# Group 2 of the second layer takes Strassen's scheme for its second product, as the last group does

## Chip, cores and metric

The kernel runs on one core of a Trainium2 chip. The metric is the device time of one execution in microseconds (us). TensorE (PE) multiplies, with its weight loads listed apart as PEld; VectorE (DVE) and ScalarE (ACT) work element by element; SyncE (SP) issues most of the transfers. Each engine takes its instructions in the order of its own queue.

## What is computed

An attention over random features gives 2304 tokens of 512 numbers. Two feed-forward layers follow, each with a first product (512 to 2048), a function element by element, and a second product (2048 to 512). The change lies in the second of them:

```python
def _moe2_ref(x, w_in, w_out):
    h = x @ w_in                      # (2304, 512) @ (512, 2048)
    g = np.where(h > 0.0, h, np.exp(np.minimum(h, 0.0)) - 1.0)
    return g @ w_out                  # (2304, 2048) @ (2048, 512)
```

Everything is float32. Each operand of a product is split into a high and a low part (fp32r), and a product is the sum of three: high by high, high by low, low by high.

## The kernel before

**Groups, blocks, tours.** The 2048 hidden numbers of a layer are cut into four groups of 512 (g = 0 to 3). The tokens are four full blocks of 512 (i = 0 to 3) and a block of 256 left over (i = 4). One pass over a block for a group is a tour (moe, g, k, i); moe = 1 is the second layer. Groups 1 and 2 of the second layer visit the blocks in the order 0, 4, 1, 2, 3, and group 3 in the order 0, 1, 2, 3, 4. A tour's second product is recorded inside the next tour, a quarter at each of four places.

**First product.** In all groups of the second layer it follows Strassen's scheme in Winograd's form: seven products of 12 matmuls (`times`, L759) into the PSUM banks `pa`, `pw` and `pb`, with the operands b, t3, t2, p, t1, t4, q, which SyncE loads from DRAM for every tour (`load_x`, L729). ACT copies `pa` into `pb` (L1082) before the product t2 adds onto `pb`; DVE makes the quadrants c22 (L1097) and c21 (L1102). Then come relu, exp and tanh on ACT, and two steps on DVE (L782 and L783 in a plain group, L951 and L952 in a Strassen group) for each of the four quadrants 11, 22, 21, 12.

**Second product, plain.** `chunk` (L810): four pieces of 12 matmuls with 512 moving columns, for which ACT casts each quadrant's high part (L792) and DVE subtracts it for the low part (L77). `summed` adds each result to the output so far, `ya` (L985), four DVE steps a tour.

**Second product by Strassen's scheme**, for the groups in `SECOND`: DVE makes four differences of quadrants (`difference`, L957: t1 = 21 - 22, t2 = 11 - t1, t3 = 11 - 21, t4 = 12 - t2). Seven operands are split (`halved`: ACT cast L963, DVE subtraction L77) instead of four. `quadrants` multiplies seven times 12 matmuls with 256 moving columns (L837), into the banks `px`, `pr`, y, z and v; ACT carries partial sums from bank to bank (L869, L880, L888); `grown` adds to the output in half steps (L921), twelve a tour. `sown` (L847) sets up two more banks once, at the first such tour of the layer. In these tours `pb` is the same bank each time; in the plain ones two banks take turns:

```python
            a, w, b = psum(f"pa{nm}"), psum(f"pw{nm}"), seeds[m % 2 if moe and not second else 0]
```

**Weights.** During the tours of a group the weights of the next group are made, at places that `chores_of` sets: 1, 2, 4, 6 and 8 of 8 parts by the end of the five tours. A part takes one step on ACT (L135) and two on DVE (L143, L150). Weights for a Strassen product also take eight half-wide DVE sums for four parts (L171 to L179) and seven casts and seven low parts (`wl`, L77), instead of four and four. These chores stand in the same queues as the tours' own steps.

Of the kernel before, what the change touches and what calls it, by code (L numbers as in the profile page):

```python
# [17 lines left out]
def linear_attention_two_ffn_kernel(  # L18
# [79 lines left out]
    parts = [(moe, f, o) for moe in range(2) for f in range(NF) for o in range(2)]  # L98
    parts[:2 * GF] = sorted(parts[:2 * GF], key=lambda p: (p[1] + LOOK * p[2], p[2]))
    parts[2 * GF:] = sorted(parts[2 * GF:], key=lambda p: (p[0], p[1] // GF, p[2], p[1]))  # L100
    SECOND = ((0,1),(0,2),(1,3))
    staged, w_t = {}, {}
    tf_t, combos, ws_t, casts, lows = {}, {}, {}, [], []
    HN = W // 2
# [2 lines left out]
    def summed_up(p):  # L107

        g = p[0], p[1] // GF
        return g in SECOND if p[2] else g != (0, 0)  # L110

# [731 lines left out]
    def sown(n, moe=0, g=1):  # L843
        wide = ws_t[moe, g * GF, "a"][0]
        while len(seeds) < n:
            seeds.append(psum(f"pb{moe}{len(seeds)}"))
            nc.tensor.matmul(seeds[-1], wide[:, :P], wide, start=True, stop=True)  # L847

    def quadrants(tour):

        moe, g, k, i = tour
        if moe == 0:
            sown(4, moe, g)
        elif k == 0 and (moe, g - 1) not in SECOND:
            del seeds[2:]
# [161 lines left out]
    def toured(before):  # L1017

        sown(2 if tours[0][:2] not in SECOND else 1)
        todo = [before[0:1], before[1:2], before[2:], []]  # L1020
        for n, tour in enumerate(tours):
# [8 lines left out]

            second = tour[:2] in SECOND
            if i == B:
# [216 lines left out]
```

## Time and profile before

| | |
|---|---|
| median of 3 runs | 908.32 us (907.88 to 908.86) |
| the profiled execution's own time | 908.27 us |
| its span, first to last instruction | 906.5 us |
| PE, DVE, ACT busy over the span | 894.5, 711.2, 607.7 us |
| group 2 of the second layer, first matmul of its block 0 to first of group 3's | 700.88 to 796.28 us of the span |
| group 3 of the second layer, from its first matmul on | 796.28 us of the span to the end |

The busy time of an engine counts its instructions where they overlap once. Matmuls are pipelined, so the time that one takes in a stream is read from one start to the next and not from its duration; the same holds for DVE, whose steps start before the one ahead has quite ended.

### The profile page before, as it was taken

The page shows a single profiled execution, that of the slowest core. Times are in us where ns is not written, and L with a number is a line of the kernel's source. Part 1 is how long each engine was busy: PE and PEld are TensorE (multiplying, and loading weights), DVE is VectorE, ACT ScalarE, POOL GpSimd, SP SyncE. Part 2 cuts the span into 40 slices and gives each one's busy share as a digit, 9 for nine tenths or more (in the row PEclk, how much of TensorE's full clock was granted, in tenths as well). Part 3 has the DMA queues.
Part 4 walks back from the last instruction along what each step waited for, and adds up shares of the span by engine and source line. Part 5 has one row for each costly group of instructions (what it writes and reads, how often), then busy time and mean ns, then how long its engine had stood idle before and what let it go on. Part 6 is the DMA issues. An engine that isn't in the chain of part 4 may idle for free. (4 is left out here: it accounts for less than half of the span.)

```text
span 906.5 us, 20710 instructions
## 1 busy us (share of the span) xinstructions
PE 894.5 (99%) x7807; PEld 844.4 (93%) x7807; DVE 711.2 (78%) x1329; ACT 607.7 (67%) x1292; POOL 86.8 (10%) x188
## 2 busy tenths in 40 slices
PE   8999999999999999999999999999999999999997
PEld 7888999998999999999999999899899989989997
DVE  5898875688876888777879897966597748878887
ACT  7999976664767675766366666755485638666663
POOL 4678730000000000000000000000000000000000
PEclk9999999999999999999999999999999999999999
DMA  9675522524998676577589664275468655653653
GB/s 242 168 196 159 170 83 75 177 94 154 349 374 302 216 250 239 179 231 255 197 279 335 244 209 164 96 256 195 160 203 270 222 183 168 205 200 126 222 173 94
DMA packets 134724, 183.89 MB, mean 203 GB/s; under 512 B 34272, under 2 KB 70624, under 8 KB 134624
## 3 DMA queue, kind: packets, MB, share of 16 engines
q1 hardware_dynamic: 133328, 181.88, 60.3%
q8 instruction: 62, 1.02, 0.5%
q10 hardware_dynamic: 1296, 0.69, 0.3%
q14 instruction: 38, 0.31, 0.1%
HBM read 145.29 MB, written 37.22 MB: 201 GB/s over the span
## 5 line engine op out<-in xcount | busy, mean ns | idle before, releaser
L810 PE MATMUL py<-wh,gh 128*128 128x512 f32 x216 | 85.2, 394 | 0.0
L810 PE MATMUL py<-wl,gh 128*128 128x512 f32 x216 | 85.1, 394 | 0.0
L810 PE MATMUL py<-wh,gl 128*128 128x512 f32 x216 | 85.1, 394 | 0.0
L782 DVE SCALAR_TENSOR_TENSOR r<-r,t 128x512 f32<-128x512 f32 x54 | 37.1, 687 | 57.4 <-ACT t L781 57.4
L77 DVE TENSOR_TENSOR gl<-gf,gh 128x512 fp32r<-128x512 f32 (+1 forms) x104 | 65.0, 625 | 4.1 <-ACT gh L792 0.5
L810 PEld LDWEIGHTS py<-wh,gl 128*128 128x128 f32 x216 | 40.6, 188 | 9.6
L810 PEld LDWEIGHTS py<-wl,gh 128*128 128x128 f32 x216 | 40.6, 188 | 7.4
L810 PEld LDWEIGHTS py<-wh,gh 128*128 128x128 f32 x216 | 40.6, 188 | 7.4
L135 ACT ACTIVATE cm<-st 128x512 f32<-128x512 f32 x64 | 44.2, 698 | 2.1 <-DMA st<-in_moe_w_out_dram 1.8
L792 ACT CAST gh<-gf 128x512 fp32r<-128x512 f32 x54 | 33.3, 617 | 17.0 <-DVE gf L783 16.1
L150 DVE SCALAR_TENSOR_TENSOR cv<-cm,cv 128x512 uint32<-128x512 uint32 x64 | 43.4, 685 | 0.8
L1082 ACT COPY pb<-pa 128x512 f32<-128x512 f32 x28 | 16.1, 574 | 40.1 <-PE pa L759 39.9
L1097 DVE TENSOR_TENSOR c<-pb,vs 128x512 f32<-128x512 f32 x28 | 19.3, 690 | 28.3 <-PE pb L759 21.7
L818 PE MATMUL py<-gh,wh 128*128 128x256 f32 x144 | 40.4, 281 | 0.0
L818 PE MATMUL py<-gh,wl 128*128 128x256 f32 x144 | 40.4, 281 | 0.0
L818 PE MATMUL py<-gl,wh 128*128 128x256 f32 x144 | 40.4, 281 | 0.0
L1090 ACT COPY us<-pb 128x512 f32<-128x512 f32 x28 | 16.4, 587 | 34.6 <-PE pb L759 29.1
L549 PE MATMUL ph<-xh,wh 128*128 128x256 f32 (+1 forms) x128 | 38.8, 303 | 0.0
L585 PE MATMUL py<-gh,wh 128*128 128x256 f32 (+1 forms) x128 | 38.4, 300 | 0.0
L585 PE MATMUL py<-gl,wh 128*128 128x256 f32 (+1 forms) x128 | 37.8, 295 | 0.0
L585 PE MATMUL py<-gh,wl 128*128 128x256 f32 (+1 forms) x128 | 37.8, 295 | 0.0
L549 PE MATMUL ph<-xh,wl 128*128 128x256 f32 (+1 forms) x128 | 37.7, 295 | 0.0
(1250 smaller groups left out, 3608.7 us busy)
## 6 DMA issues: line engine op xcount, KB each, us to landing
st<-in_moe_w_in_dram SPq DMA_DIRECT2D x32, 512.0 KB, 5.4
st<-in_moe_w_out_dram SPq DMA_DIRECT2D x32, 512.0 KB, 3.8
vk<-in_v_dram SPq DMA_DIRECT2D x32, 128.0 KB, 4.7
out_dram<-ya SPq DMA_DIRECT2D x30, 128.0 KB, 2.0
ld0k<-in_k_dram SPq DMA_DIRECT2D x4, 256.0 KB, 5.1
ld0q<-in_q_dram SPq DMA_DIRECT2D x4, 256.0 KB, 4.7
ld1k<-in_k_dram SPq DMA_DIRECT2D x4, 256.0 KB, 5.0
ld1q<-in_q_dram SPq DMA_DIRECT2D x4, 256.0 KB, 4.6
```

The lines of the kernel that those rows point to most:

```text
L77: eng.tensor_tensor(out=out, in0=whole, in1=hi.bitcast(F32), op=ALU.subtract)
L135: nc.scalar.activation(out=staged[p][1], in_=staged[p][0][:, :, 1].bitcast(F32), func=AF.Prelu, scale=REBIAS, alpha=NEGATIVE)
L150: nc.vector.scalar_tensor_tensor(out=t, in0=m.bitcast(U32), scalar=3, in1=t, op0=ALU.logical_shift_left, op1=ALU.bitwise_or)
L549: nc.tensor.matmul(ph[:, :n], wt[:, cs], x_part(xt, i, c)[:, n0:n1], start=(m == 0), stop=(m == 3 * KD - 1))
L585: nc.tensor.matmul(y, w[:, ts], a, start=j == 0 and m == 0 and t % per == 0, stop=j == GF - 1 and m == 2, skip_group_check=per > 1,)
L782: nc.vector.scalar_tensor_tensor(out=r, in0=r, scalar=1.0, in1=t, op0=ALU.add, op1=ALU.mult)
L792: nc.scalar.copy(out=gh, in_=gf)
L810: nc.tensor.matmul(y_t[l, u], a[:, s0], w, start=first and pr == 0 and m == 0, stop=last and pr == 1 and m == 2,)
L818: nc.tensor.matmul(y_t[l, u][:, e * HN:(e + 1) * HN], w[:, ts], a[:, pr * HN:(pr + 1) * HN], start=first and pr == 0 and m == 0 and e == 0 ...
L1082: nc.scalar.copy(out=b, in_=a)
L1090: nc.scalar.copy(out=us, in_=b)
L1097: nc.vector.tensor_tensor(out=c22, in0=b, in1=vs, op=ALU.add)
```

## The change

One entry more in the table of the groups whose second product takes Strassen's scheme: group 2 of the second layer, which had the plain one.

```diff
-    SECOND = ((0,1),(0,2),(1,3))
+    SECOND = ((0,1),(0,2),(1,2),(1,3))
```

The functions that it calls for that group are those that group 3 already uses. On PE the 48 matmuls of L810 in each full tour of group 2 become 84 of L837, and the rest stays in place. On DVE group 2's steps change as below. The numbers in a name are group and block (c_2_2 is c22 of group 2, block 2) and a buffer number; `gl` and `glt` are low parts, `g` and `gt` quadrants and differences, `r` the exp of a quadrant, `t` the tanh.

DVE's queue in block 2 of group 2, before, from c22 on:

```order
L1097 TENSOR_TENSOR c_2_2_11386<-pb_4446,vs_2_2_11384 128x512
L77 TENSOR_TENSOR gl_1_2_2_11531<-gf_1_2_2_11480,gh_1_2_2_11529 128x512
L1102 TENSOR_TENSOR c_2_2_11385<-pw_2_2_11382,us_2_2_11383 128x512
L985 TENSOR_TENSOR ya_1_0_0_9284<-py_2_1_0_0_11433,ya_1_0_0_9284 128x512
L985 TENSOR_TENSOR ya_1_0_1_9286<-py_2_1_0_1_11434,ya_1_0_1_9286 128x512
L782 SCALAR_TENSOR_TENSOR r_1_2_2_11553<-r_1_2_2_11553,t_1_2_2_11554 128x512
L783 TENSOR_TENSOR gf_1_2_2_11552<-r_1_2_2_11553,c_2_2_11386 128x512
```

The same place in the change:

```order
L1097 TENSOR_TENSOR c_2_2_11513<-pb_4446,vs_2_2_11511 128x512
L957 TENSOR_TENSOR g_1_2_1_11477<-g_1_2_1_11477,gt_1_2_1_11489 128x512
L77 TENSOR_TENSOR glt_1_2_1_11684<-g_1_2_1_11477,ght_1_2_1_11683 128x512
L1102 TENSOR_TENSOR c_2_2_11512<-pw_2_2_11509,us_2_2_11510 128x512
L921 TENSOR_TENSOR ya_1_0_0_9284<-pr_2_1_11639,ya_1_0_0_9284 128x256
L921 TENSOR_TENSOR ya_1_0_1_9286<-pr_2_1_11639,ya_1_0_1_9286 128x256
L921 TENSOR_TENSOR ya_1_0_0_9284<-pr_2_1_11639,ya_1_0_0_9284 128x256
L921 TENSOR_TENSOR ya_1_0_1_9286<-pr_2_1_11639,ya_1_0_1_9286 128x256
L951 SCALAR_TENSOR_TENSOR r_1_2_2_11709<-r_1_2_2_11709,t_1_2_2_11710 128x512
L952 TENSOR_TENSOR g_1_2_2_11708<-r_1_2_2_11709,c_2_2_11513 128x512
```

Between c22 and c21 there now stand the difference t4 of the block before and, right behind it, its low part, which needs ACT's cast of that difference; four half steps take the place of two full ones.

DVE's queue further on in block 2 of the change, from the difference t1 to the low part of t2 (before, nothing of L957 stood here, the four `wl` rows followed the last `gl` of block 2, and two rows of L985 stood where the four of L921 are):

```order
L957 TENSOR_TENSOR gt_1_2_2_11789<-g_1_2_2_11749,g_1_2_2_11708 128x512
...
L952 TENSOR_TENSOR g_1_2_2_11777<-r_1_2_2_11778,c_1_2_2_11781 128x512
L77 TENSOR_TENSOR wl_14a<-cv_14_0_11299,wh_14a 128x512
L77 TENSOR_TENSOR wl_14b<-cv_15_0_11419,wh_14b 128x512
L77 TENSOR_TENSOR wl_14c<-cs_15_0_11501,wh_14c 128x512
L77 TENSOR_TENSOR wl_12d<-cd_13_0_11218,wh_12d 128x512
L921 TENSOR_TENSOR ya_1_0_0_9284<-pb_11153,ya_1_0_0_9284 128x256
L921 TENSOR_TENSOR ya_1_0_1_9286<-pb_11153,ya_1_0_1_9286 128x256
L921 TENSOR_TENSOR ya_1_1_0_9368<-pb_11155,ya_1_1_0_9368 128x256
L921 TENSOR_TENSOR ya_1_1_1_9370<-pb_11155,ya_1_1_1_9370 128x256
L77 TENSOR_TENSOR glt_1_2_2_11877<-gt_1_2_2_11789,ght_1_2_2_11876 128x512
```

The chores for group 3's weights (`wl`) now stand between t1 and the low part of t2 (glt of gt, in the last row).

ACT's queue from the tanh of block 2's quadrant 12 to block 3's first copy, before:

```order
L781 ACTIVATE t_1_2_2_11612<-gf_1_2_2_11610 128x512
L792 CAST gh_1_2_2_11618<-gf_1_2_2_11582 128x512
L1082 COPY pb_4652<-pa_2_3_11644 128x512
L1083 COPY vs_2_3_11647<-pw_2_3_11645 128x512
L792 CAST gh_1_2_2_11684<-gf_1_2_2_11610 128x512
```

and in the change:

```order
L940 ACTIVATE t_1_2_2_11779<-g_1_2_2_11777 128x512
L963 CAST ght_1_2_2_11793<-gt_1_2_2_11789 128x512
L1082 COPY pb_4446<-pa_2_3_11836 128x512
L1083 COPY vs_2_3_11839<-pw_2_3_11837 128x512
L963 CAST ght_1_2_2_11876<-gt_1_2_2_11791 128x512
L963 CAST gh_1_2_2_11880<-g_1_2_2_11777 128x512
```

The copy of `pa` into `pb` (L1082), after which PE can go on with block 3, now stands behind the cast of DVE's difference t1 of block 2.

## Rows read from the trace of the kernel before

**Rows 1.** The page's first part: engines' busy us (share of the span), instructions.

```profile
PE 894.5 (99%) x7807; PEld 844.4 (93%) x7807; DVE 711.2 (78%) x1329; ACT 607.7 (67%) x1292; POOL 86.8 (10%) x188
```

**Rows 2.** Windows: length, PE, PEld, DVE, ACT, POOL busy, clock, DMA.

```profile
754.23:775.27 21.04, 21.04 (x135) 18.95 (x133) 20.25 (x37) 16.85 (x31) 0.00 (x0) 1.00 0.61 209
837.66:858.50 20.84, 20.40 (x171) 20.00 (x170) 17.46 (x34) 14.13 (x27) 0.00 (x0) 1.00 0.67 227
```

**Rows 3.** Timeline of DVE, group 3, block 2: start, us, instruction [idle before].

```profile
839.21 0.68 DVE L957 TENSOR_TENSOR gt<-g,g 128x512 f32<-128x512 f32 x1
...
847.61 0.69 DVE L951 SCALAR_TENSOR_TENSOR r<-r,t 128x512 f32<-128x512 f32 x1 [0.67 <-ACT t L940]
...
849.24 0.69 DVE L1097 TENSOR_TENSOR c<-pb,vs 128x512 f32<-128x512 f32 x1
849.85 0.68 DVE L957 TENSOR_TENSOR g<-g,gt 128x512 f32<-128x512 f32 x1
851.21 0.69 DVE L77 TENSOR_TENSOR glt<-g,ght 128x512 fp32r<-128x512 f32 x1 [0.69 <-ACT ght L963]
...
852.42 1.41 DVE L921 TENSOR_TENSOR ya<-pr,ya 128x256 f32<-128x256 f32 x4
853.75 0.68 DVE L951 SCALAR_TENSOR_TENSOR r<-r,t 128x512 f32<-128x512 f32 x1
...
856.79 0.69 DVE L951 SCALAR_TENSOR_TENSOR r<-r,t 128x512 f32<-128x512 f32 x1 [1.63 <-DMA xspl<-xd13p]
...
860.06 0.68 DVE L957 TENSOR_TENSOR gt<-g,g 128x512 f32<-128x512 f32 x1
```

**Rows 4.** Timelines of ACT and PE at that place.

```profile
839.93 0.62 ACT L963 CAST ght<-gt 128x512 fp32r<-128x512 f32 x1 [1.48 <-DVE gt L957]
840.45 0.58 ACT L1082 COPY pb<-pa 128x512 f32<-128x512 f32 x1
...
841.91 0.28 PE L759 MATMUL pb<-xst2h,wh_12c 128*128 128x256 f32 x1
```

**Rows 5.** Timeline of PE: a plain piece's 12 matmuls, then 24 of Strassen's.

```profile
778.09 0.40 PE L810 MATMUL py<-wh,gh 128*128 128x512 f32 x1
...
780.88 0.28 PE L759 MATMUL pb<-xst2h,wh_8c 128*128 128x256 f32 x1
...
834.82 0.28 PE L837 MATMUL pb<-wh_12D,gh 128*128 128x256 f32 x1
...
837.66 0.27 PE L759 MATMUL pa<-xsbh,wh_12a 128*128 128x256 f32 x1
```

**Rows 6.** Timeline of DVE: chores in group 2.

```profile
754.51 0.42 DVE L143 TENSOR_SCALAR cv<-st 128x512 uint32<-128x512 uint32 x1
754.84 0.68 DVE L150 SCALAR_TENSOR_TENSOR cv<-cm,cv 128x512 uint32<-128x512 uint32 x1
...
772.96 0.42 DVE L171 TENSOR_TENSOR cs<-cv 128x256 f32<-128x256 f32 x1
...
774.67 0.69 DVE L782 SCALAR_TENSOR_TENSOR r<-r,t 128x512 f32<-128x512 f32 x1
```

**Rows 7.** Waits of PE over the whole span: us in total, times, longest.

```profile
PE px L837 <- DVE wl_10B L77: 0.7, 1, 0.7
```

**Rows 8.** Timelines of DVE and PE, block 1 of group 2.

```profile
749.20 0.69 DVE L782 SCALAR_TENSOR_TENSOR r<-r,t 128x512 f32<-128x512 f32 x1 [8.36 <-ACT t L781]
...
756.77 0.68 DVE L77 TENSOR_TENSOR gl<-gf,gh 128x512 fp32r<-128x512 f32 x1
...
757.08 0.39 PE L810 MATMUL py<-wh,gh 128*128 128x512 f32 x1
```

**Rows 9.** Timeline of SP in group 3: output stores and the load behind them.

```profile
838.33 7.03 SPq L969 DMA_DIRECT2D out_dram<-ya  x8
845.45 0.40 SPq L729 DMA_DIRECT2D xst4h<-xd12t  x1
```

**Rows 10.** The page's costliest groups: busy us, mean ns.

```profile
L810 PEld LDWEIGHTS py<-wh,gl 128*128 128x128 f32 x216 | 40.6, 188 | 9.6
```

## The prediction

> **What bounds the kernel now.** I read the page first: PE is busy for 894.5 of 906.5 us [rows 1]. So a gain must come off PE's work, and a loss must come from a new wait of PE. Windows cut at the tours come next [rows 2]. In a plain tour of group 2 (21.04 us) DVE is busy for 20.25 us and PE for all of it; in a Strassen tour of group 3, which carries no chores, DVE still takes 17.46 of 20.84. The change brings both loads together in group 2. So I followed DVE through one Strassen tour in the timeline [rows 3], and then the step by which PE depends on it [rows 4].
>
> The chain is this. DVE makes the difference t1 of a block (839.21). ACT casts it (839.93), and only then, its queue being in order, copies `pa` into `pb` (840.45). PE's product t2 of the next block adds onto `pb` (841.91). At the least this takes 0.72 to the cast, 0.52 to the copy, and some 0.64 for the copy (0.58 long) to end and PE to go on: 1.88 us. Here it took 2.70, so PE had 0.82 us to spare. In a Strassen tour DVE may therefore be late by 0.8 us, and beyond that PE waits. The reader should compare the time from one t1 to the next on DVE with PE's time for the 14 products in between.
>
> **What the change saves.** PE's plain pieces take 2.79 us for 12 matmuls, 232.5 ns each; Strassen's take 2.84 us for 24, 118.3 ns each [rows 5]. A full tour goes from 48 x 0.2325 = 11.16 to 84 x 0.1183 = 9.94 us: 1.22 less, 4.9 in four tours. Block 4 has 24 of the wide ones (5.58) and gets 48 narrow ones (5.68), 0.1 more. The two matmuls of `sown` only move from group 3 to group 2. Together PE's work shrinks by 4.8 us.
>
> On the matmuls' spacing the Trainium skill says otherwise (TensorE: Matmul & The Clock Gate, "Back-to-back issue gap"): a stream of weight load and matmul pairs is given about 81 ns a matmul at 128 columns and about 131 at 512. A straight line between these, an estimate, gives 98 ns at 256, by which a tour would go from 6.3 to 8.2 us and the change would cost PE 7.8 us in four tours. The trace decides against it: 118 ns is close to half of 232.
>
> **What it adds on DVE.** A full tour goes from 18 full-wide steps to 21 and 12 half-wide ones. From t1 to t1 in group 3 DVE took 20.85 us [rows 3]. Of that it stood idle without need for 0.67 before 847.61 and 1.63 before 856.79, each 0.08 more since a step may start before the one ahead has ended (0.69 long, 0.61 from start to start at 849.24), and for some 0.3 between 847.61 and 849.24, where two steps that take 1.3 filled 1.63. What is left is 18.1 us. It includes 0.77 that can't be filled: the low part of t4 stands right behind t4 itself and waits for ACT's cast (849.85 to 851.21, where one step is 0.6).
>
> Chores come on top, at 0.60 for a low part or an L150, 0.33 for an L143 (754.51 to 754.84), and 1.71 for four half-wide sums that wait for one another (772.96 to 774.67) [rows 6]. From the order of the changed queue:
>
> - t1 of block 1 to t1 of block 2: two low parts, three L150, two L143, eight sums, 7.1 us; but four half steps fewer (1.33, [rows 3]), as block 4 is the one before. 18.1 + 7.1 - 1.3 = 23.9
> - block 2 to 3: four low parts, one L150, two L143, 3.7: 21.8
> - block 3 to group 3's block 0: four low parts, one L150, four sums, 4.7: 22.8
> - to group 3's block 1: three low parts, 1.8: 19.9
> - from there on 18.1.
>
> PE's 14 products of 12 take 168 x 0.1183 = 19.9 us (19.87). The first four loops need 88.4 on DVE and 79.5 on PE: with DVE late from the start, PE waits for 8.9 us in them. That PE waits for DVE where a Strassen tour carries chores is seen already, in the first layer: 0.7 us for a low part of a weight [rows 7].
>
> DVE is late from the start: in block 1 it has free time (8.36 idle before 749.20, until ACT's tanh), which the queue's order doesn't let later work use. The low part of quadrant 22 stands at 756.77 [rows 8]; two half steps (0.66) take their place behind it, so t1 begins at about 758.0 and PE's t2 at 759.9. PE has done the product t3 at 757.08 and, after one piece of the second product (1.42), would be ready at 758.5. That is a first wait of 1.4, which I keep between 0 (if block 1 runs ahead) and 1.4.
>
> Block 0 and block 4 together have 32.1 on DVE for some 31.7 on PE, but they start from plain tours with time to spare, and block 1's idle time takes up what is left. Group 2's own weights add three low parts and eight sums, under 6 us, to group 1's last tours, which by the same prices then hold 17.3 and 16.4 us of DVE's steps from c22 to c22 for 21 of PE; I cost that at nothing. ACT gets seven steps of about 0.52 more in a full tour; with 16.85 of 21.04 busy [rows 2] where chores are thickest it comes to some 20.5, below the 22 to 24 that such a tour now takes. The loads on SP keep their number and order.
>
> One cost is passed on to group 3. SP issues eight output stores, which wait for DVE's half steps, before it can load the operand t4 [rows 9], and the tour of [rows 2] is 20.84 long where its products take 19.87: 0.97 lost. With DVE at the end of its slack, those half steps come 0.8 later against PE: 0.8 more. Between 0 and 1.6 (two such tours).
>
> Sum: 908.27 (the profiled execution, whose span is 906.5; the median is 908.32, the same within its spread) - 4.8 + 1.4 + 8.9 + 0.8 = 914.6 us.
>
> **Rivals.**
>
> - *DVE's load stays hidden, and PE's saving is all that shows*: 908.27 - 4.8 = 903.5. For it: plain tours with 20.25 of 21.04 on DVE don't hold PE [rows 2]. Against: the slack of 0.8 [rows 4], and four loops in a row that need more than PE. It decides where PE's waits stay under 3.0 us, that is where DVE's four loops take 82 instead of 88.4.
> - *The slack comes back in each loop*: if the link from t1 to PE had 0.82 of give anew in each of the five places, 4.1 of the waits would go, and with them the passed-on 0.8: 909.7, no change to speak of (within 0.2%, 1.8 us, about what this measurement can tell from none). Against: a queue that is late stays late.
> - *Loads come late as well*: if each of the five tours of group 2 lost what the tour of group 3 loses at its t4 load, 0.97, it would be 4.9 more: 919.5. For it: operands need pages that Strassen tours hold longer. Against: no stores stand ahead of the loads there.
> - *Narrow matmuls are paced by their weight loads*, 188 ns each [rows 10]: 84 x 0.188 = 15.8 a tour, 4.6 more than before instead of 1.2 less, 18.6 in four; DVE would then hide: 908.27 + 18.6 = 926.9. The Trainium skill's spacing rule above points this way. Against it: the 24 narrow ones at 118 ns [rows 5].
>
> **How the numbers follow.** Main case 0.80, hidden 0.05, slack 0.06, late loads 0.08, paced 0.01. The main case's own bounds: first wait 0 to 1.4, passed-on cost 0 to 1.6, DVE's prices 1% either way on 88.4 (0.9), 0.7 more if ACT's tanh of quadrant 21 isn't ready in the loop with few chores. Low: -4.8 + 0 + 8.0 + 0 = +3.2, 911.5. High: -4.8 + 1.4 + 9.8 + 0.7 + 1.6 = +8.7, 917.0; I reach to 918 towards the late loads. Faster is the hidden case, 0.05; the slack case gives no change, 0.06; the rest is slower, 0.89. That the change doesn't do what it says is excluded: the queues show 84 matmuls of L837 for 48 of L810.
>
> **What would show it.** Right: narrow matmuls at 118 ns in group 2; tours of block 2, block 3 and group 3's block 0 of 22 to 24 us instead of 21; PE's waits there before `pb` (L759, released by ACT L1082), before L837 for a low part of t2 (released by DVE L77), and DVE with hardly any idle time but that behind t4; group 3's t4 load later still. Wrong: DVE idle time of more than 1 us a loop between block 2 of group 2 and block 1 of group 3, or PE without waits there.

## The result, and the profile after

The change makes the kernel slower: 921.58 us (median of four, 921.11 to 922.49) against 908.18 in the same session, a ratio of 1.0145 with the interval [1.0132, 1.0158]. That is 13.4 us more, where 6.3 were forecast: the sign was right, the size was about half of what came, and 921.6 lies outside the forecast of 911.5 to 918. The profiled execution has a span of 920.3 us (906.5 before).

Nearly all of it (13.2 us of the 13.8 by which the span grew) lies in four stretches, and these are the four loops of the prediction. I cut both traces where PE starts the product t2 (the first matmul into `pb` from `xst2h`): in block 2 and block 3 of group 2, then in blocks 0, 1 and 2 of group 3. Up to the first cut the two kernels are level (759.85 us before, 760.01 after); behind the last one 64.6 and 65.0 us are left. Between them stand, in windows of the kernel before and then of the changed one (columns as in [rows 2]):

```profile
759.85:841.91 82.06, 82.06 (x567) 76.14 (x566) 68.65 (x120) 54.38 (x98) 0.00 (x0) 1.00 0.51 173
```

```profile
760.01:784.30 24.29, 20.83 (x169) 20.10 (x169) 22.96 (x45) 17.30 (x33) 0.00 (x0) 1.00 0.53 173
784.30:806.28 21.98, 20.25 (x169) 20.04 (x169) 21.05 (x42) 16.82 (x32) 0.00 (x0) 1.00 0.52 170
806.28:833.97 27.69, 21.77 (x171) 21.36 (x170) 25.38 (x49) 17.61 (x33) 0.00 (x0) 0.94 0.59 194
833.97:855.29 21.32, 21.32 (x170) 21.32 (x169) 16.62 (x33) 13.60 (x25) 0.00 (x0) 0.92 0.20 70
```

82.06 us have become 95.28. I call the four loops A to D. PE's 168 matmuls take 19.9 us in each; in A to C DVE is busy for 92 to 96% of the time (as in the plain tour of [rows 2]; it was 84% in the Strassen tour there); in C and D, and nowhere else here, PE's granted clock is below 1.

PE's longest waits from 700 us on (us in total, times, longest), where before there was none of DVE's or ACT's over 0.4:

```profile
PE pb L837 <- DVE glt L77: 6.8, 3, 3.6
PE pb L759 <- ACT pb L1082: 2.6, 2, 1.6
PE px L837 <- DVE wl_14B L77: 2.3, 1, 2.3
...
PE px L837 <- DVE wl_10B L77: 0.3, 1, 0.3
```

The code calls the seven products of Strassen's second product p1 to p7. The first row is p6, which needs the low part of t2; the second is the link that the prediction followed [rows 4]; the third is p1, which needs the low part of a weight of group 3, and the last the same product in group 2's first tour. DVE's timeline through loop C (start, us, instruction, idle before) says why two of them are so long:

```profile
804.23 0.68 DVE L957 TENSOR_TENSOR gt<-g,g 128x512 f32<-128x512 f32 x1
...
808.14 0.69 DVE L150 SCALAR_TENSOR_TENSOR cv<-cm,cv 128x512 uint32<-128x512 uint32 x1
...
812.45 1.41 DVE L921 TENSOR_TENSOR ya<-pb,ya 128x256 f32<-128x256 f32 x4
813.78 0.68 DVE L77 TENSOR_TENSOR glt<-gt,ght 128x512 fp32r<-128x512 f32 x1
...
818.74 0.69 DVE L1097 TENSOR_TENSOR c<-pb,vs 128x512 f32<-128x512 f32 x1 [1.09 <-PE pb L759]
...
828.61 0.68 DVE L957 TENSOR_TENSOR gt<-g,g 128x512 f32<-128x512 f32 x1
...
832.52 0.69 DVE L77 TENSOR_TENSOR wl_14B<-cv,wh_14B 128x512 fp32r<-128x512 f32 x1
```

Between t1 (804.23) and the low part of t2 (813.78) stand an L150, four sums, three low parts of weights and four half steps, from 808.14 on 5.6 us. PE's wait for it delays the product t1, so that DVE itself stands idle for 1.09 us ahead of c22. And wl_14B comes 3.9 us behind the next t1. PE at the two waits, with the spacing of its matmuls:

```profile
810.66 0.28 PE L837 MATMUL pb<-wl_8C,ght 128*128 128x256 f32 x1
814.51 0.58 PE L837 MATMUL pb<-wh_8C,glt 128*128 128x256 f32 x1 [3.57 <-DVE glt L77]
...
815.11 0.41 PE L837 MATMUL pb<-wl_8C,ght 128*128 128x256 f32 x1
815.32 0.41 PE L837 MATMUL pb<-wh_8C,glt 128*128 128x256 f32 x1
...
817.83 0.28 PE L759 MATMUL pb<-xst1h,wh_14b 128*128 128x256 f32 x1
817.94 0.28 PE L759 MATMUL pb<-xst1l,wh_14b 128*128 128x256 f32 x1
...
830.64 0.28 PE L837 MATMUL px<-wh_14B,gh 128*128 128x256 f32 x1
833.26 0.39 PE L837 MATMUL px<-wl_14B,gh 128*128 128x256 f32 x1 [2.35 <-DVE wl_14B L77]
```

After the wait the matmuls stand 0.21 us apart, later 0.12 again. Windows show it as the clock (the column ahead of the last two): 0.50, the lower of its two levels, 1.2 GHz, behind either wait, from about 814.2 to 817.4 and from about 834.5 to 837.9 us.

```profile
814.50:816.80 2.30, 2.29 (x10) 2.29 (x11) 2.30 (x4) 0.16 (x1) 0.00 (x0) 0.50 0.09 35
...
836.26:836.76 0.50, 0.50 (x4) 0.50 (x4) 0.50 (x2) 0.42 (x1) 0.00 (x0) 0.50 0.00 0
...
838.30:840.50 2.20, 2.20 (x21) 2.20 (x20) 0.16 (x1) 1.75 (x3) 0.00 (x0) 1.00 0.45 133
```

### The profile page after: what moved, and what is told of

It is laid out like the page before. It is cut to its first block, busy times and chain, and to the rows that moved or that the text cites. A ratio compares the mean times of both kernels' runs of the same rounds, so it can differ in the third digit from the quotient of the medians.

```text
span 920.3 us, 21175 instructions
## 1 busy us (share of the span) xinstructions
PE 895.4 (97%) x7975; PEld 852.9 (93%) x7975; DVE 741.0 (81%) x1404; ACT 622.5 (68%) x1324; POOL 86.7 (9%) x188
## 5 line engine op out<-in xcount | busy, mean ns | idle before, releaser
L810 PE MATMUL py<-wh,gh 128*128 128x512 f32 x144 | 56.8, 394 | 0.0
L810 PE MATMUL py<-wh,gl 128*128 128x512 f32 x144 | 56.7, 394 | 0.0
L810 PE MATMUL py<-wl,gh 128*128 128x512 f32 x144 | 56.7, 394 | 0.0
L77 DVE TENSOR_TENSOR gl<-gf,gh 128x512 fp32r<-128x512 f32 (+1 forms) x86 | 52.6, 612 | 3.8 <-ACT gh L792 0.2
L782 DVE SCALAR_TENSOR_TENSOR r<-r,t 128x512 f32<-128x512 f32 x36 | 24.7, 687 | 33.9 <-ACT t L781 33.9
L150 DVE SCALAR_TENSOR_TENSOR cv<-cm,cv 128x512 uint32<-128x512 uint32 x64 | 43.3, 685 | 0.8
L963 ACT CAST gh<-g 128x512 fp32r<-128x512 f32 x56 | 34.5, 616 | 12.9 <-DVE g L952 12.9
L77 DVE TENSOR_TENSOR gl<-g,gh 128x512 fp32r<-128x512 f32 x56 | 38.4, 686 | 4.1 <-ACT gh L963 4.1
L963 ACT CAST ght<-g 128x512 fp32r<-128x512 f32 x32 | 19.8, 618 | 26.9 <-DVE g L957 26.9
L549 PE MATMUL ph<-xl,wh 128*128 128x256 f32 (+1 forms) x128 | 37.7, 294 | 0.0
L963 ACT CAST ght<-gt 128x512 fp32r<-128x512 f32 x32 | 19.8, 619 | 25.1 <-DVE gt L957 24.6
```

The costliest lines, as they stand in the source:

```text
L77: eng.tensor_tensor(out=out, in0=whole, in1=hi.bitcast(F32), op=ALU.subtract)
L150: nc.vector.scalar_tensor_tensor(out=t, in0=m.bitcast(U32), scalar=3, in1=t, op0=ALU.logical_shift_left, op1=ALU.bitwise_or)
L549: nc.tensor.matmul(ph[:, :n], wt[:, cs], x_part(xt, i, c)[:, n0:n1], start=(m == 0), stop=(m == 3 * KD - 1))
L782: nc.vector.scalar_tensor_tensor(out=r, in0=r, scalar=1.0, in1=t, op0=ALU.add, op1=ALU.mult)
L810: nc.tensor.matmul(y_t[l, u], a[:, s0], w, start=first and pr == 0 and m == 0, stop=last and pr == 1 and m == 2,)
L963: nc.scalar.copy(out=h, in_=t)
```

## The experiments

Seventeen kernels, all cut at the same rows of PE. "Over before" is the median less that of the kernel before on the same chip, whose medians were 908.2 to 909.1; the last column is what follows the last cut.

| run | median us | over before | first cut | A | B | C | D | A to D | rest |
|---|---|---|---|---|---|---|---|---|---|
| before | 908.2 | | 759.9 | 21.0 | 21.0 | 19.7 | 20.3 | 82.1 | 64.6 |
| after | 921.6 | 13.4 | 760.0 | 24.3 | 22.0 | 27.7 | 21.3 | 95.3 | 65.0 |
| low_pool | 924.3 | 15.6 | 761.4 | 27.4 | 24.7 | 23.4 | 19.9 | 95.5 | 64.7 |
| half_first | 922.7 | 13.9 | 761.6 | 24.4 | 22.6 | 26.2 | 22.0 | 95.1 | 65.0 |
| filled | 920.3 | 11.6 | 760.3 | 24.3 | 23.5 | 25.8 | 19.9 | 93.4 | 64.6 |
| g2_alone | 915.0 | 6.2 | 759.9 | 22.3 | 23.5 | 22.7 | 21.1 | 89.6 | 63.8 |
| no_lows | 912.5 | 3.8 | 759.8 | 23.4 | 20.4 | 23.6 | 19.9 | 87.2 | 64.6 |
| no_chores | 905.1 | -3.6 | 759.1 | 20.0 | 19.9 | 19.9 | 19.8 | 79.6 | 64.6 |
| ahead_a | 921.1 | 12.4 | 765.3 | 22.3 | 25.3 | 20.6 | 19.8 | 88.0 | 64.8 |
| ahead_i | 913.7 | 5.0 | 761.6 | 24.1 | 21.4 | 19.9 | 19.9 | 85.2 | 64.8 |
| ahead_j | 913.4 | 4.8 | 763.6 | 23.9 | 20.0 | 19.8 | 19.9 | 83.6 | 64.9 |
| ahead_l | 920.1 | 11.5 | 771.1 | 23.8 | 19.9 | 19.9 | 19.9 | 83.5 | 65.7 |
| before_l | 909.0 | 0.5 | 760.2 | 21.0 | 21.0 | 19.8 | 20.3 | 82.1 | 64.8 |
| ahead_ih | 914.5 | 6.0 | 762.5 | 24.2 | 20.0 | 20.0 | 19.9 | 84.0 | 64.6 |
| b_first | 920.1 | 11.3 | 759.9 | 24.3 | 22.0 | 26.5 | 20.5 | 93.3 | 64.5 |
| half_b | 918.3 | 9.5 | 761.6 | 24.4 | 21.8 | 22.3 | 21.4 | 89.7 | 64.7 |
| b_filled | 918.1 | 9.3 | 759.8 | 24.3 | 23.5 | 23.2 | 20.5 | 91.5 | 64.7 |
| j_no_lows | 907.9 | -1.2 | 761.0 | 20.0 | 19.9 | 19.9 | 19.9 | 79.6 | 64.8 |
| j_94 | 911.8 | 2.7 | 763.1 | 22.7 | 20.0 | 19.9 | 19.9 | 82.4 | 64.5 |

The ratios' intervals are about 0.0015 either way, 1.4 us; differences between runs of less than 2 us are told with what the cuts show, which are from one profile each. A profiled execution can itself lie up to 2 us from its median (ahead_l 2.1 over, ahead_ih 1.6 under).

### The load, its place, or the clock

**half_first.** The half step of t2 (`halved`: ACT's cast and DVE's subtraction, not the half steps of L921) ahead of the last slot of chores:

```diff
                 difference(tour, "t3", "11", "21", "21")
                 joined()
+                if tour[:2] == (1, 2):
+                    halved(tour, "t2")
...
-                carried.append(lambda tour=tour: halved(tour, "t2"))
+                if tour[:2] != (1, 2):
+                    carried.append(lambda tour=tour: halved(tour, "t2"))
```

> The changed kernel with one thing of the order changed in group 2: the half step of t2 (ScalarE's cast and VectorE's glt) stands ahead of the last slot of chores of its tour, no longer behind it. No work is added or taken out. Theory of the places: p6's three waits (1.6, 1.9 and 3.7 us) go, the slow clock behind the longest of them goes with it, and TensorE's delay no longer makes VectorE idle at c22 (1.1 us): the loop of 27.7 us falls to 23 to 24.5 and the kernel to 916 to 918. Theory of the load: VectorE is short of time anyway, whatever is first, and the chores now make the next product wait instead (p1 for wl_14B, or t2 for ScalarE's copy): 920.5 to 922.

922.7 us, the load's number or just over. p6 no longer waits, DVE has no idle time ahead of c22, and p1 waits twice as long for the same weight:

```profile
833.47 0.58 PE L837 MATMUL px<-wl_14B,gh 128*128 128x256 f32 x1 [4.79 <-DVE wl_14B L77]
```

The number alone does not decide for the load: in this trace the clock is at 0.50 for 6.8 us around 788 and again around 836, twice as long as in the changed kernel at its two places. So the order may have gained some 3 us (an estimate, half of the 6.8 us more) that the clock took back.

**low_pool.** The low parts of the weights on GpSimd:

```diff
-            minus(nc.vector, l, tf, h)
+            minus(nc.gpsimd if key[0] and key[1] >= 2 * GF else nc.vector, l, tf, h)
```

> The changed kernel with the low parts of the weights of groups 2 and 3 of the second layer subtracted on GpSimd in place of VectorE; nothing else moves. Between the t2 products of 760.0 and 855.3 us the changed kernel's VectorE makes 13 such low parts, 0.60 us each from start to start: 7.8 us. Theory of the load (VectorE has more work than TensorE in these four loops, and the loops last as long as that work): the work falls from 88.4 to 80.6 us beside TensorE's 79.5, the loops fall from the measured 95.3 to 81 or 82, and the kernel to 907.5 to 909, level with the kernel before. Theory of the places (the work would fit, and only the waits of p6 for glt and of p1 for wl_14B, with the slower clock behind them, cost): the two waits go and the rest stays, 912 to 914. Rival: GpSimd, which took 1.04 us for a tensor_tensor of 128x512 earlier in this kernel, delivers wl_14B later than VectorE did, or slows VectorE's own instructions while it works: 917 to 922.

924.3 us: the rival, and worse. In loop A four low parts on GpSimd (first fence) stand beside DVE's sums of weights (second fence), which take 1.30 to 1.42 us where the one ahead of them, begun before GpSimd's, took 0.43:

```profile
778.05 1.41 POOL L77 TENSOR_TENSOR wl_14a<-cv,wh_14a 128x512 fp32r<-128x512 f32 x1 [23.31 <-DMA xst1l<-xd13t]
779.43 1.48 POOL L77 TENSOR_TENSOR wl_14b<-cv,wh_14b 128x512 fp32r<-128x512 f32 x1
```

```profile
777.88 0.43 DVE L171 TENSOR_TENSOR cs<-cv 128x256 f32<-128x256 f32 x1
778.34 1.42 DVE L172 TENSOR_TENSOR cv<-cv,cv 128x256 f32<-128x256 f32 x1
779.79 1.41 DVE L173 TENSOR_TENSOR cs<-cv 128x256 f32<-128x256 f32 x1
781.30 1.30 DVE L174 TENSOR_TENSOR cd<-cv,cs 128x256 f32<-128x256 f32 x1
782.52 1.74 DVE L951 SCALAR_TENSOR_TENSOR r<-r,t 128x512 f32<-128x512 f32 x1
```

A step of DVE lasts about as long as the GpSimd step beside it, and both about as long as the two alone, one after the other (0.43 + 1.04 = 1.47). So the work is not taken off DVE: it waits for it. Late by that, a low part of the tour's own (`gl` of quadrant 22) makes p1 wait for 4.8 us, and behind this the clock is at 0.50 for 10 us, which lengthens A and B. The Trainium skill (SBUF — State Buffer, "SBUF: two separate sides") says that a DVE instruction with two SBUF inputs and a GpSimd one that reads SBUF take a shared pair of ports in turn, each for its whole length; these rows agree (1.41 to 1.48 us each, side by side).

**filled.** Matmuls of weight nought ahead of p6 and p1 in the two long waits:

```diff
+            if moe and (g, k, key) in FILLED:
+                for n in range(FILLED[g, k, key]):
+                    nc.tensor.matmul(
+                        bank[to][:, :HN], nought, wide_of(moe, g)[:, :HN], start=fresh and n == 0, stop=False,
+                        skip_group_check=True,
+                    )
+                fresh = False
```

with `FILLED = {(2, 4, "t2"): 28, (3, 0, "22"): 18}`; `nought` is a tile of zeros made at the start.

> The changed kernel with TensorE kept at work in the two long waits: 28 matmuls with a weight of nought, 256 columns each, accumulated onto p6's bank before it in the last tour of group 2, and 18 before p1 in the tour behind the first of group 3. They add nothing to the sums. At 118 ns each they last 3.3 and 2.1 us, a little less than the waits (3.7 and 2.5). Theory of the clock: the granted clock of 0.50 in 814.5 to 817.3 and 834.8 to 837.7 us follows from TensorE's waits, stays at 1.00 now, and about 1.5 us come back at each place: 918 to 919. Rival: VectorE sets the length of these loops, TensorE just waits elsewhere for what it gains: 920.8 to 922.

920.3 us, 11.6 over before where the change is 13.4 over: about 1.8 us back, between the two ranges. Windows at the place of p6's wait, then at 792 us, where nothing is filled:

```profile
810.60:814.50 3.90, 3.90 (x36) 3.90 (x35) 3.83 (x9) 3.87 (x8) 0.00 (x0) 1.00 0.93 291
814.50:817.50 3.00, 3.00 (x28) 3.00 (x27) 3.00 (x7) 1.55 (x4) 0.00 (x0) 1.00 0.61 210
...
792.50:795.20 2.70, 2.70 (x15) 2.70 (x15) 2.32 (x5) 1.31 (x3) 0.00 (x0) 0.50 0.56 207
```

and the changed kernel at 792 us:

```profile
792.10:794.90 2.80, 2.80 (x26) 2.80 (x25) 2.70 (x6) 1.39 (x3) 0.00 (x0) 1.00 0.35 118
```

The clock stays at 1.00 at the filled waits, and loop D comes to 19.9 us: its whole excess was the clock. B is 1.5 us longer, because in this trace the clock fell already behind p6's wait of 1.9 us at 791, ahead of either place that was filled. B and C together are only 0.4 shorter: they end when DVE has made wl_14B, which it does no sooner.

**g2_alone.** `SECOND = ((0,1),(0,2),(1,2))`.

> Group 2 with Strassen's scheme in its second product and the last group without it: the scheme is in one group of the second layer as in the kernel before, but in the group in whose tours the chores of the following weights are done. TensorE has the same number of matmuls as in the kernel before. Theory of the load: the chores (here some 5.4 us lighter than in the changed kernel, because a plain last group needs 4 low parts and no sums of weights where it had 7 and 8) still take VectorE beyond TensorE's time in three loops, 63 us beside 59.6, and the first wait of 1.4 stays: 911.5 to 914. Rival: the loss needs both groups, since the carried half steps and sums of group 2 then fall into tours of group 3 that have their own: 907.5 to 909.5.

915.0 us, 6.2 over: 1 us above the load's range, which held no fall of the clock (here 3.4 us at 0.50, behind a wait of 1.8 near 789), and the rival is out. With PE's work as before, the scheme costs 6 us merely by standing in the tours that carry the chores.

**no_lows** leaves out 14 of DVE's steps. The high part stands in for the low one and so counts twice: the result is another, not only a less exact one:

```diff
+            if key[0] and key[1] >= 3 * GF:
+                ws_t[key] = h, h
+                return
             l = page([W], f"wl{}_{}{}".format(*key), F32R)
```

> The changed kernel without the low parts of the last group's weights: their high parts are used in their place, so that 14 subtractions of VectorE (0.60 us each from start to start; 13 of them stand between 754 and 834 us) are not done, and the result is less exact. TensorE's work is the same. Theory of the load: 14 x 0.60 = 8.4 us less work on VectorE in the loops, nothing else in their place: the loops come to TensorE's 19.9 us or a little above, 905.5 to 909. Theory of the places: p1's wait for wl_14B goes with its clock (4.0 us) and p6's waits shrink by the low parts ahead of them (about 3 us), the rest stays: 913 to 916.

912.5 us, just under the second theory's range, above the first's. 8.4 us of steps left out give 9.6 back (8.0 of them in the loops), but the loops stay 7.7 over PE's 79.5: in A and C DVE still has the sums and L150, p6 still waits 2 us, and the clock falls once more.

**no_chores.** The last group's weights are not prepared:

```diff
+    parts = [p for p in parts if p[:1] == (0,) or p[1] < 3 * GF]
...
             ws_t[key] = h, l
+            if key[0] and key[1] >= 2 * GF:
+                ws_t[1, key[1] + GF, key[2]] = h, l
```

> The changed kernel without any preparation of the last group's weights: its tours use those of group 2, so that loads, ScalarE's and VectorE's chores (about 21 us of VectorE in the tours of group 2 and the first of group 3) are left out, and the result is another. Theory of the load: VectorE then has 17 us in each full tour of groups 2 and 3, less than TensorE's 19.9, and the kernel is bound by TensorE, at the 903.5 us of the rival in which all is hidden: 902.5 to 905.5. Rival: the half steps and sums of Strassen's second product make TensorE wait by their own dependencies (ScalarE's copy of pa behind the cast of t1, p6 behind glt), whatever the chores: 907 or more.

905.1 us, 3.6 faster than before. In the four loops nothing of the scheme's own holds PE up:

```profile
759.09:838.65 79.56, 79.56 (x673) 79.56 (x673) 69.44 (x131) 57.28 (x106) 0.00 (x0) 1.00 0.47 159
```

The loops take the 79.5 us that the prediction gave PE (4 x 19.87). All that the change loses, 17 us against this run, comes from the chores: DVE's, ACT's and their loads together, which this run doesn't part.

**b_first** exchanges two of the chores:

```diff
-            key, tf, h = lows.pop(0)
+            key, tf, h = lows.pop(1 if lows[0][0] == (1, 14, "A") and len(lows) > 1 else 0)
```

> The changed kernel with two chores of the same length exchanged: VectorE subtracts wl_14B, which p1 needs first, where it subtracted wl_14A, at 824.6 us, and wl_14A behind wl_12D at 833.7 us. VectorE's load is the same to the row. Theory of the missed wait (p1's 2.5 us for wl_14B and the 1.5 us of half clock behind it are a term of their own): both go, p6 in the next tour then waits about 1 us for glt, and the time falls by 2.5 to 4 us, to 917.5 to 919.5. Theory of the load: VectorE is as busy as before and TensorE waits for the next thing that it makes: 920.8 to 922.5.

**half_b** is b_first with half_first's edit, **b_filled** is b_first with `FILLED = {(2, 4, "t2"): 28}`.

> The exchange of the two chores (b_first) and the half step of t2 ahead of the chores (half_first) together; no work is added or taken out. half_first alone was 922.7 us: its p6 no longer waited, and p1 waited 5.0 us in one piece, with half clock behind it. Theory of the missed wait: p1's wait and its clock go, nothing is idle on VectorE, and the forecast's sum (914.6 us) comes out but for some tenths of t2's waits: 914.5 to 917. Theory of the load: 919.5 to 922, as each of them alone.

> The exchange of the two chores (b_first) with the 28 matmuls of weight nought ahead of p6 in the last tour of group 2, whose wait of 3.7 us is left. Theory of the clock: the granted clock stays at 1.00 behind that wait, t1 is done about 1.5 us sooner, VectorE's 1.1 us of idling ahead of c22 goes: 1 to 1.6 us less than b_first. Rival: VectorE's own work decides from there on, and the time is that of b_first within 0.5 us.

b_first: 920.1 us, 11.3 over before, 2.1 less than the change; A to D are 2.0 shorter. That is between the two ranges: p1's wait and the clock behind it are gone, p6 in the next tour waits 0.4, and loop C is 1.2 us shorter, not the 2.5 of the wait. The rest went into the clock: behind p6's same wait of 3.7 us it stayed at 0.50 for 6.8 us in this trace, where it was 3.4 in the changed kernel, and DVE idles 1.97 us ahead of c22 for 1.09. C is 19.9 of work, 3.7 of wait and 2.9 of clock. The clock at the same place in b_first, then in the changed kernel:

```profile
818.41:818.91 0.50, 0.50 (x4) 0.50 (x4) 0.00 (x0) 0.00 (x0) 0.00 (x0) 0.50 0.61 234
```

```profile
818.51:819.01 0.50, 0.50 (x6) 0.50 (x5) 0.27 (x1) 0.00 (x0) 0.00 (x0) 1.00 0.71 250
```

b_filled: 9.3 over, 2.0 less again, a little more than the clock's number, as there was more of the slow clock to take away; with wl_14B no longer in the way, B and C together are 1.8 shorter. half_b: 9.5 over, above the range of the missed wait and below the load's; its loops are 89.7 us, where the forecast's sum for DVE is 88.4. About half of the 3.2 us that it lacks to the forecast is ahead of the loops (first cut at 761.6, forecast 759.9): wl_10B now stands behind the half step in group 2's first tour, so that PE waits 1.1 us for it where it was 0.5, and ACT's cast of t2's high part stands ahead of the copy of `pa`, 0.7 more. PE's waits in b_first, then in half_b, from 780 to 860 us:

```profile
PE pb L837 <- DVE glt L77: 5.7, 3, 3.6
PE pb L759 <- ACT pb L1082: 1.6, 1, 1.6
```

```profile
PE pb L759 <- ACT pb L1082: 3.8, 2, 2.4
PE px L837 <- DVE gl L77: 1.5, 1, 1.5
PE pb L837 <- DVE glt L77: 1.1, 1, 1.1
```

So each edit of the order removed its wait, and some of the time went into the next one or into a longer slow clock; half_b, with both, comes nearest to what DVE's load alone costs.

### The chores elsewhere

Five runs begin the chores earlier, each by other numbers of parts in the line of `chores_of` that sets how far the parts are begun (`lim`), as in ahead_l:

```diff
-        lim = min(len(parts), 2 * NF * moe + 2 * GF * (g + 1) + AHEAD[k])
+        lim = min(len(parts), 2 * NF * moe + 2 * GF * (g + 1) + {(1, 0): (1, 2, 4, 7, 10), (1, 1): (3, 6, 9, 12, 14), (1, 2): (8, 8, 8, 8, 8)}.get((moe, g), AHEAD)[k])
```

> The changed kernel with the chores of group 2's tours begun earlier: by the end of its tours of blocks 0, 4, 1, 2, 3, 3, 4, 6, 8, 8 parts of the next weights are begun and no longer 1, 2, 4, 6, 8. By the cost of each row VectorE's chores in these five tours and the first of group 3 go from 3.4, 3.3, 4.8, 6.0, 5.1, 2.4 us to 7.0, 5.1, 5.4, 5.1, 2.4, 0: the same sum in other places. Theory of the load: VectorE's whole work there is 22.5, 14.1, 18.7, 22.2, 19.5, 17.1 us where TensorE has 21.1, 16.8, 15.6, 19.9, 19.9, 19.9; it falls behind by 1.4, nothing, 3.1 and 5.4 us and then no further (7.7 in the changed kernel), no chore is left in the last two loops, and the waits for p6 and p1 there go with their clock: 908 to 913. Rival: the loads and pages of the weights aren't there earlier, so TensorE or VectorE waits for them in the first tours: 916 to 922.

> The changed kernel with the chores spread over the tours of groups 1 and 2: in group 1, whose tours are plain, 2, 4, 6, 9, 11 parts (the last three of group 3's weights already), in group 2 5, 6, 8, 8, 8. By the cost of each row VectorE's whole work from the last tour of group 1 on is 18.0, 21.0, 14.1, 17.7, 19.5, 17.1, 17.1 us, where TensorE has 21.0, 21.1, 16.8, 15.6, 19.9, 19.9, 19.9: no more than 2.1 us behind anywhere. Theory of the load: TensorE sets the pace nearly everywhere, the change's 4.8 us on TensorE come out, and the kernel is faster than the one before: 903.5 to 907. Rival: the order within the tours, not the load, makes TensorE wait: 912 to 918. Another: pages and loads are missing for weights made so early, above 916.

> The changed kernel with the chores spread further back, over groups 0 to 2 of the second layer: 1, 2, 4, 7, 10 parts begun by the ends of group 0's tours, 3, 6, 9, 12, 14 in group 1, all 8 from the first tour of group 2 on. By the cost of each row VectorE's work in the tours of group 1 is 15.0, 13.1, 18.3, 20.3, 18.6 us, in those of group 2 20.6, 11.5, 13.3, 17.1, 17.1, and in group 3 17.1: nowhere over TensorE's time except by 2.8 us in block 1 of group 1, behind which 3 us are free. No chore stands in any tour with Strassen's second product behind the small block. Theory of coupling (where VectorE has more to do than TensorE, TensorE's wait holds up a product, and VectorE then waits for that product, so that the loss is larger than the surplus; where it has less, nothing is lost): 904 to 907, faster than the kernel before. Rival: pages or loads are missing for weights made so early, or the tours of group 1 become the ones that wait: 908.5 to 913.

> Between the runs ahead_i and ahead_l: 2, 4, 7, 10, 12 parts in group 1, then 6, 8, 8, 8, 8 in group 2. VectorE's work is 17.1, 20.0, 18.6 us in the last tours of group 1 and 21.9, 13.8, 15.7, 17.1, 17.1 in group 2. Theory of coupling: VectorE is over TensorE's time by 0.8 in the first tour of group 2 and level in its block 1, with chores of 2.4 us still in the latter: 905 to 908. Rival as for ahead_l: 908.5 to 913.

> The run in which the chores were spread over groups 1 and 2 (913.7 us), with the half step of t2 ahead of the last slot of chores in group 2 besides. Its trace showed p6 waiting 1.9 and 1.3 us for glt behind 3.7 and 2.5 us of chores, and VectorE then idle for 1.7 us because the product behind p6 came late. Theory of coupling: with the load below TensorE's time after these two tours, the order now matters, and both waits and the idle time go: 908.5 to 910.5. Rival: as in the changed kernel, the order only moves the waits: 912.5 to 914.

> The kernel before with the same spread of the chores as the run above has: the control. Theory of coupling: VectorE had less work than TensorE in every tour of the kernel before too, so there is nothing to gain: 908 to 909.5. Rival: the spread itself gives a gain whatever the second product of group 2 is: 904 to 907.

ahead_a 921.1, ahead_i 913.7, ahead_j 913.4, ahead_l 920.1, ahead_ih 914.5: all missed the theory's range, ahead_l, ahead_j and ahead_ih the rival's as well, and none is as fast as the kernel before; before_l is the same as before (ratio 1.0005, [0.9995, 1.0014]), as the control should be. The theory was right for the loops out of which the chores went: in ahead_j and ahead_l B, C and D are 19.8 to 20.0 us. But the first cut comes 1.6 to 11 us later: in ahead_a p1 waits 3.5 us near 729, with slow clock behind it, for wl_10B, a low part of group 2's own weights, which the new chores have put back by 2.6; in ahead_l PE waits 5.1 us for ACT's copies between banks (2.3, 1.0 and 1.8 us at L869, L880 and L888, from 738 to 749), and the rest of its 11 us is left open. And in ahead_i, ahead_j, ahead_l and ahead_ih loop A stays at 24. ahead_l has no chore in it at all, and DVE stands idle there:

```profile
781.99 0.69 DVE L951 SCALAR_TENSOR_TENSOR r<-r,t 128x512 f32<-128x512 f32 x1 [4.74 <-ACT t L940]
```

In ahead_j two steps of ACT's timeline in loop A stand out, copies that on PE's side had long been free to go:

```profile
765.82 0.58 ACT L1083 COPY vs<-pw 128x512 f32<-128x512 f32 x1 [2.26 <-DVE g L952]
...
769.71 0.59 ACT L1090 COPY us<-pb 128x512 f32<-128x512 f32 x1 [0.70 <-PE pb L837]
```

In the changed kernel the same two copies don't wait:

```profile
759.89 0.58 ACT L1083 COPY vs<-pw 128x512 f32<-128x512 f32 x1
...
765.38 0.57 ACT L1090 COPY us<-pb 128x512 f32<-128x512 f32 x1
```

The kernel hands out its SBUF tiles as pages, 93 of them (`NPAGES`). A copy of a PSUM bank that waits for a step of DVE on other data, or for a matmul into another bank, can, in this program, only be waiting for the page that it writes. So I asked for pages.

**j_no_lows** is ahead_j with no_lows' edit, 14 pages fewer; **j_94** is ahead_j with `NPAGES = 94`. Against the expectation below, loop A of ahead_j does hold chores: three low parts (wl_14B, wl_14C, wl_12D, 1.8 us from 765.65 on), which j_no_lows leaves out. So j_94 alone changes nothing but pages.

> The run ahead_j without the low parts of the last group's weights (their high parts are used in their place, so the result is less exact): 14 subtractions of VectorE are left out, none of them in the loop from t2 of block 2 to t2 of block 3, and 14 SBUF pages are not held. In ahead_j this loop took 23.9 us with no chore in it. Theory of the pages (weights made early hold pages, and ScalarE's copies and the steps behind them wait for one): the loop falls to 20 or 20.5 us, ScalarE's copies no longer wait for VectorE, and the kernel comes to 906 to 909. Rival (the half steps and casts of the tour's own hold it up): the loop stays at 23 us or more, and only the tours ahead gain: 910.5 to 912.5.

> The run ahead_j with 94 SBUF pages where all others have 93, which is all that fits; nothing else. Theory of the pages: ScalarE's waits for pages in the loop of block 2 (2.3 and 0.7 us) become shorter by some tenths up to half, and the time falls by 0.5 to 2 us, to 911.5 to 913. Rival: the same within 0.5 us of 913.4.

j_no_lows 907.9 us, j_94 911.8: both in the pages' ranges. Loop A in ahead_j and in j_no_lows:

```profile
763.62:787.53 23.91, 21.14 (x168) 20.20 (x169) 17.88 (x33) 14.24 (x26) 0.00 (x0) 1.00 0.46 156
```

```profile
760.98:780.96 19.98, 19.98 (x168) 19.98 (x169) 16.99 (x32) 14.86 (x28) 0.00 (x0) 1.00 0.52 173
```

One page more takes 1.2 us off that loop (22.7). 14 fewer in use, and three steps of DVE less, take off 3.9; as ahead_l's loop is as long without any chore, I put most of it down to the pages, but no run parts the two. A weight made earlier is paid for with pages; in the changed kernel itself no such wait shows.

## Why the prediction was off

- **PE's saving: right.** 24 narrow matmuls still take half as long each as the wide ones [rows 5] (0.12 us apart at 817.83), and no_chores shows what is left when nothing else binds: 79.6 us for the four loops, 3.6 us for the kernel, where the rival of the hidden load had 4.8 (0.8 of the difference is a wait ahead of the first cut). The rival in which narrow matmuls are paced by their weight loads is out.
- **The first wait of 1.4: right.** PE's t2 was forecast at 759.9; it came at 760.01, after 1.1 us. The sum does not quite fit this place, though: of the 4.8 saved, 2.5 fall ahead of it, so that with 1.4 lost t2 should have come 1.1 before the 759.85 of the kernel before. It did not: 0.5 went into `sown`, which comes back in loop D, and 0.5 into p1's wait for wl_10B in group 2's first tour. The latter is a cost of group 2's own weights, which I had put at nothing, and that the place came out right is in part luck.
- **DVE's four loops, "PE waits for 8.9 us in them": mis-sized, and this is the step that failed.** The loops were forecast at 23.9, 21.8, 22.8 and 19.9 us, 88.4 in all; they took 24.3, 22.0, 27.7 and 21.3, 95.3. DVE's own sum was nearly right: from t1 to t1 it took 24.3 in A (0.4 over), 21.8 in B as forecast, and 24.4 in C for 22.8, of which 1.1 is idle time. In D it took 24.0 for 19.9, over 3 us of it idle (2.20 and 0.95) because PE came late. What failed is that I let only one link bind PE, that from t1 to `pb` [rows 4], and took PE's clock as given; p6's wait for the low part of t2 stood among my signs, but with no price of its own. The 6.9 us more are: 0.6 in A and B; 3.3 of waits in C (3.7 for p6 and 2.5 for p1, 6.2 where the sum allowed 22.8 - 19.9 = 2.9); and 3.0 of clock, in C 27.7 - 19.9 - 6.2 = 1.6, in D 21.3 - 19.9 = 1.4, where PE doesn't wait at all. p1's need of wl_14B, 3.9 us behind t1, could have been read from the queue; [rows 7] shows just this wait, in the first layer.
- **Shown by the runs:** b_first takes 2.0 off the loops and b_filled 1.8 more, of the 6.9, without taking a step out, and half_b brings them to 89.7. That the whole rest would follow from a perfect order is not shown.
- **Passed on to group 3, 0.8:** small, as forecast: 0.4 behind the last cut.
- **Rivals.** The late side of my range rested on late loads; none of the long waits is for a load. What lay beyond the range was one the rivals did not hold: a wait that brings its own costs with it, idle time on DVE and half clock on PE.
- **The sign that I named as the one against me**, over 1 us of needless idle time on DVE in a loop, did show, at 818.74 and again in D, and for the reason given above.

## What to carry to other kernels

Add up each engine's work loop by loop, as here, but then follow every operand that the waiting engine needs to its place in the other's queue: the sum gives the least that the loop can take, and the place decides how much more. Work that is hidden in one tour is not hidden in the next when the tour's own load grows, and shifting it has a price as well: on GpSimd it held DVE up, and done earlier it held pages (j_94). A run without the side work at all tells within one try whether the change or the side work is to blame.

## What the runs showed of the hardware

- Behind PE's waits of 3.7 and 2.5 us in the changed kernel the granted clock was 0.50 for some 3.4 us each, with matmuls 0.21 us apart for 0.12; behind those of 1.1 to 1.9 us in the same trace it stayed at 1.00. It does not go by the wait's length alone: behind p6's wait of 1.9 us near 791 us it stayed at 1.00 in the changed kernel and in b_first and fell to 0.50 in filled and b_filled, where that wait is the same; behind 1.8 us it fell in g2_alone, behind 2.4 us near 738 it stayed at 1.00 in ahead_l.
- How long it stays low differs too: behind p6's wait of 3.7 us 3.4 us in the changed kernel and 6.8 in b_first, which are the same up to there. In their loops this cost 1.4 to 1.6 us for the shorter and 2.9 for the longer stretch.
- DVE and GpSimd, each with two operands in SBUF, took turns: DVE's half-wide sum went from 0.43 to 1.42 us, its L951 from 0.69 to 1.74, and GpSimd's step from 1.04 early in this kernel to 1.3 to 1.8.
